# Attention on one core: the store of each pair in two halves of 64 rows, on both sides of the V load

## The chip, the core and the metric

The kernel runs on one core of a Trainium2 chip. The metric is the device time of one execution in microseconds (us), lower is better. Times shown are those of the unprofiled runs; a profiled execution has a time of its own, and its trace is where durations come from.

## What is computed

Attention with grouped heads, in bfloat16. 16 batches, 32 query heads of 16 positions, 8 key/value heads of 2048 positions, 128 elements per head; four query heads share one key/value head. Cut to what matters:

```
B, Hq, Hkv, Sq, Sk, D = 16, 32, 8, 16, 2048, 128
scores = einsum("bhqd,bhkd->bhqk", q, k) * D ** -0.5
out = einsum("bhqk,bhkd->bhqd", softmax(scores), v)
```

There are 16 x 8 = 128 key/value heads, each with 4 x 16 = 64 query rows. K and V together are 128 MB of input; the output is 2 MB.

## The kernel before

Two key/value heads make a *pair* p, 64 pairs in all: 128 query rows, and so 128 rows of output. All data is moved by DMAs that one engine, SP (SyncE), issues from its own queue. A DMA is cut into packets that 16 DMA engines move; each engine works through its own ring in the order of the issues. For a pair, SP issues

- K (`load_k`, issue at L187): 1 MB into one of 6 buffers `Kn`, in rows of 8 KB; before that it waits (`sem_kt`) until VectorE has transposed the pair that used the buffer;
- V (`load_v`, L195): 1 MB into one of 8 buffers `Vb`, in rows of 4 KB; before that it waits (`sem_pv`) for the product with V of the pair that used the buffer. The last pair's V comes in three pieces (L200), so that its product can begin early;
- the store (`store`, L213): 128 rows of 256 B, 32 KB, from one of 8 buffers `Osb` (in the profile `O`) to the output; before that it waits (`sem_nm`) until ACT has written the buffer;
- for every four pairs Q (`load_q`, L208), 128 KB.

The engines' part in a pair: VectorE (DVE) transposes K's blocks into `KT` (L343), takes the scores from PSUM with their minimum (L361) and the reciprocal of the sum of a row (L352). TensorE (PE) makes the scores (L274, L233), transposes the exponentials (L285) and multiplies by V (L302). ScalarE (ACT) takes the exponential (L391), copies the transposes out of PSUM (L401), and *norms* (L411): it scales the product by the reciprocal into `Osb`. Before a norm that reuses a buffer of `Osb`, ACT waits (`sem_o`) until the store from it, eight pairs earlier, has landed. GpSimd spreads Q (L176).

SP's order is written out by hand: a loop over steps t = 0 to 76. In step t it issues K of pair t, now and then Q, V of pair t-5 (`VLAG`), and the store of pair t-12 (`SLAG`):

```
for t in range(NP + SLAG + 1):
    if t < NP:
        load_k(t)
...
    if 0 <= t - VLAG < NP:
        load_v(t - VLAG)
    if 0 <= t - SLAG < NP:
        store(t - SLAG)
```

From step 64 on there is no K load left, from step 69 on no V load: the last eight steps hold stores only. At the very end SP waits until all stores have landed (L226). Each DMA adds 16 to its semaphore when it is complete, one for each of the 16 DMA engines.

Of the kernel before, what the change touches and what calls it, by code (L numbers as in the profile page):

```python
# [15 lines left out]
NO = 8  # L16
# [5 lines left out]
SLAG = 12  # L22
# [4 lines left out]
def bass_standalone__gqa_softmax__sampling_kernel(  # L27
# [11 lines left out]
    NP = G // 2  # L39
# [21 lines left out]
    Osb = [sb(f"O{i}", [128, 128], BF16) for i in range(NO)]  # L61
# [13 lines left out]
    sem_o = [sem(f"sem_o{i}") for i in range(NO)]  # L75
# [9 lines left out]
    sem_nm = sem("sem_nm")  # L85

    qf = q.rearrange("b h s d -> (b h s) d")
    of = out.rearrange("b h s d -> (b h s) d")
# [64 lines left out]
    def stage_ap(what):  # L153
        x = what[2] if what[0] == "P" else 2
        return ST_ps[:, 512 * x:512 * (x + 1)]

    def o_ap(p):
        if p < NP - 3:
            return O_ps[:, 0:128]
        x = p - (NP - 3)  # L160
        return S_ps[:, 512 * x:512 * x + 128]

    with nc.Block() as block:

        @block.gpsimd
        def _(gp):
            gp.iota(iota_t[:, :], [[1, 128]], base=0, channel_multiplier=-1).then_inc(sem_id, 1)
            gp.wait_ge(sem_id, 1)
            gp.tensor_scalar(ident[:, :], iota_t[:, :], 0.0, None, op0=ALU.is_equal).then_inc(sem_id, 1)
            gp.tensor_scalar(ident4[:, :], iota_t[:, :], 0.0, None, op0=ALU.is_equal).then_inc(sem_id, 1)  # L170
            for c in range(NQC):
                gp.wait_ge(sem_q[c % NQ], 16 * (c // NQ + 1))
                if c >= 1:
                    gp.wait_ge(sem_st, last_q[c - 1, 1] + 1)
                src = Qn[c % NQ][:, :, :].rearrange("p j (b x) -> p (j b) x", b=2)
                gp.tensor_copy(  # L176
                    Q4[:, :, :, :, :].rearrange("p j b r x -> p (j b) r x"),
                    src.unsqueeze(2).to_broadcast([128, 2 * QPAIRS, 4, 64]),
                ).then_inc(sem_q4, 1)

        @block.sync
        def _(sp):
            def load_k(p):
                s = p % NK
                if p >= NK:
                    sp.wait_ge(sem_kt, p - NK + 1)
                sp.dma_start(Kn[s][:, :], kf[p]).then_inc(sem_k[s], 16)  # L187

            def load_v(p):
                s = p % NV  # L190
                if p >= NV:
                    sp.wait_ge(sem_pv, p - NV + 1)
                if p < NP - 1:
                    dst = Vb[s][:, :, :, :].rearrange("a g j d -> a g (j d)")
                    sp.dma_start(dst, vf[:, 2 * p:2 * p + 2, :]).then_inc(sem_v[s], 16)  # L195
                    return
                for x, (lo, hi) in enumerate(zip(CUTS, CUTS[1:])):
                    dst = Vb[s][:, :, lo:hi, :].rearrange("a g j d -> a g (j d)")
                    src = vf[:, 2 * p:2 * p + 2, D * lo:D * hi]
                    sp.dma_start(dst, src).then_inc(sem_vl[x], 16)  # L200

            def load_q(c):
                s = c % NQ
                if c >= NQ:
                    sp.wait_ge(sem_q4, c - NQ + 1)
                rows = 128 * QPAIRS
                src = qf[rows * c:rows * (c + 1), :].rearrange("(a j) d -> a j d", j=QPAIRS)
                sp.dma_start(Qn[s][:, :, :], src).then_inc(sem_q[s], 16)  # L208

            def store(p):  # L210
                s = p % NO
                sp.wait_ge(sem_nm, p + 1)
                sp.dma_start(of[128 * p:128 * (p + 1), :], Osb[s][:, :]).then_inc(sem_o[s], 16)  # L213

            for t in range(NP + SLAG + 1):
                if t < NP:
                    load_k(t)
                for c in range(NQC):
                    if t == max(c, QPAIRS * c - QLEAD):
                        load_q(c)  # L220
                if 0 <= t - VLAG < NP:
                    load_v(t - VLAG)
                if 0 <= t - SLAG < NP:
                    store(t - SLAG)
            for s in range(NO):
                sp.wait_ge(sem_o[s], 16 * (NP // NO))  # L226

        @block.tensor
        def _(pe):
# [11 lines left out]
            def emit(op, at, v_at):  # L241

                if op[0] == "QT":
                    _, c, b, u = op
                    if b == 0:
                        pe.wait_ge(sem_q4, at(QPAIRS * c, QPAIRS))
# [6 lines left out]
                    ins.then_inc(sem_st, 1)  # L253
                elif op[0] == "S":
                    _, p = op
                    pe.wait_ge(sem_kt, at(p + 1))
                    if p >= 1:
# [19 lines left out]
                    ins.then_inc(sem_s, 1)  # L277
                elif op[0] == "PT":
                    _, p, h, u = op
                    if h == 0:  # L280
                        pe.wait_ge(sem_exp, at(p + 1))
# [91 lines left out]
        @block.scalar  # L373
        def _(act):
            for op in act_prog:
                if op[0] == "qe":
                    _, c, b, u = op
                    act.wait_ge(sem_st, u + 1)
                    if c >= 2 and b == 0:
                        act.wait_ge(sem_s, QPAIRS * (c - 1))  # L380
                    act.activation(  # L381
                        QT[c % 2][:, b, :].rearrange("p (a j) -> p a j", j=QPAIRS),
                        stage_ap(op).rearrange("p (j a) -> p a j", j=QPAIRS), ACT.Copy,
                    ).then_inc(sem_ev, 1)
                elif op[0] == "exp":
                    _, p = op
                    act.wait_ge(sem_max, p + 1)
                    if p >= 2:
                        act.wait_ge(sem_st, last_p[p - 2, 1] + 1)

                    act.activation(  # L391
                        P[p % 2][:, :].bitcast(BF16).rearrange("p (n y e) -> p n y e", n=16, e=2),
                        Sneg[p % 2][:, :].rearrange("p (n e y) -> p n y e", n=16, e=2), ACT.Exp,
                        bias=nbias[:, p:p + 1], scale=-1.0, accum_out=rowsum[:, p:p + 1],
                    ).then_inc(sem_exp, 1)
                elif op[0] == "pe":
                    _, p, h, u = op
                    act.wait_ge(sem_st, u + 1)
                    if h == 0 and p >= NPT:
                        act.wait_ge(sem_pv, p - NPT + 1)  # L400
                    act.activation(  # L401
                        PT[p % NPT][:, 4 * h:4 * (h + 1), :].rearrange("p t q -> p (t q)"),
                        stage_ap(("P", p, h)), ACT.Copy,
                    ).then_inc(sem_ev, 1)
                else:
                    _, p = op
                    act.wait_ge(sem_pv, p + 1)
                    act.wait_ge(sem_rec, p + 1)
                    if p >= NO:
                        act.wait_ge(sem_o[p % NO], 16 * (p // NO))  # L410
                    act.activation(Osb[p % NO][:, :], o_ap(p), ACT.Copy,  # L411
                                   scale=rrec[:, p:p + 1]).then_inc(sem_nm, 1)

# [27 lines left out]
```

## Time and profile before

| what | value |
|---|---|
| median of 3 runs | 341.77 us (341.57 to 341.88) |
| the profiled execution | 342.24 us |
| its span, from the first to the last instruction | 340.5 us |
| busy: DVE, PE, ACT, POOL | 295.3, 278.8, 267.0, 31.8 us |
| read from HBM, written to it | 136.31 MB, 2.10 MB |
| mean rate | 407 GB/s over the span |
| K, V, Q, store: median from issue to landing | 15.9, 16.4, 15.5, 15.4 us |

How to read what follows: PE, PEld, DVE, ACT, POOL and SP are the engines (PEld are TensorE's weight loads); a q behind the name (SPq) means the engine's queue of instructions. L187 is line 187 of the kernel before. `Vb<-in_v_dram` is a DMA from the input v into a buffer Vb; `x64` is a number of instructions. A row of tenths has 40 digits, one for each fortieth of the span, and 9 means 90% or more. q1 is the queue row in which all of SP's DMAs are; q8 and q14 carry the program's own instructions. The chain of waits is followed back from the last instruction: at each step to what released it. The trace also keeps a record of each DMA packet (start, duration, bytes), and of the time at which each DMA engine told a semaphore that its share had landed (here called landing records).

### The profile page before, as it was taken

The numbers are of one execution on the slowest core, as the hardware profiler recorded it, in microseconds if no ns is written. First come the engines' busy times: TensorE is split into PE (matmuls) and PEld (weight loads), VectorE is DVE, ScalarE is ACT, GpSimd is POOL, SyncE is SP. The second block draws the span as 40 slices with busy tenths as digits, with TensorE's granted clock in tenths as the row PEclk, the third lists the DMA queues.
The fourth block names the chain that finished last, engine by engine and source line by source line (L and its number), as shares of the span: only waits on it lengthen the run. The fifth ranks groups of instructions, "written<-read, shape, count | busy, mean of one in ns | idle before, by whom it ended". The sixth has DMA issues, their size and how long they took to land.

```text
span 340.5 us, 9888 instructions
## 1 busy us (share of the span) xinstructions
PE 278.8 (82%) x4736; PEld 161.6 (47%) x3712; DVE 295.3 (87%) x320; ACT 267.0 (78%) x353; POOL 31.8 (9%) x23
## 2 busy tenths in 40 slices
PE   0687999999998787888788797897878878888885
PEld 0233555555465445445355354454454454454454
DVE  2489999999999988989989889889889889899860
ACT  1178889999888786877878877887878869778785
POOL 3202020202010020200202011020200202000000
PEclk9979999999999999999999999999999999999999
DMA  8999999999999999999999999999999999999996
GB/s 295 398 418 416 410 414 409 414 415 415 416 418 415 416 417 417 415 419 417 416 418 412 420 418 413 420 416 417 420 413 418 414 416 420 419 415 420 416 409 205
DMA packets 38705, 138.63 MB, mean 407 GB/s; under 512 B 11552, under 2 KB 14112, under 8 KB 30496
## 3 DMA queue, kind: packets, MB, share of 16 engines
q1 hardware_dynamic: 38688, 138.43, 100.7%
q8 instruction: 8, 0.13, 0.2%
q14 instruction: 9, 0.07, 0.1%
HBM read 136.31 MB, written 2.10 MB: 407 GB/s over the span
## 4 chain that ended last, share of the span: by engine, by line
DMA 58%; DVE 16%; SPq 10%; issue 7%; PE 6%; ACT 1%; POOL 1%
DMA Vb<-in_v_dram 52%; DVE KT L343 11%; SPq L187 7%; DVE Sneg L361 5%; DMA Kn<-in_k_dram 5%; PE O_ps L302 3%; SPq L213 2%; DMA Qn<-in_q_dram 1%; ACT O L411 1%; PE S_ps L274 1%; PE S_ps L233 1%; SPq L195 1%; PE ST_ps L252 1%; POOL Q L176 1%; SPq L200 0%
## 5 line engine op out<-in xcount | busy, mean ns | idle before, releaser
L343 DVE STREAM_TRANSPOSE KT<-Kn 128x1024 f32<-128x1024 f32 x128 | 151.5, 1222 | 28.7 <-DMA Kn<-in_k_dram 28.7
L391 ACT ACTIVATE P<-Sneg,nbias 128x2048 bf16<-128x2048 f32 x64 | 159.6, 2493 | 6.0 <-DVE Sneg L361 6.0
L361 DVE TENSOR_SCALAR_CACHE_REDUCE Sneg<-S_ps 128x2048 f32<-128x2048 f32 x64 | 144.4, 2256 | 7.1 <-PE S_ps L233 7.1
L274 PE MATMUL S_ps<-KT,QT 32*64 32x512 bf16 x1024 | 105.7, 393 | 6.7 <-DVE Sneg L361 5.1
L233 PE MATMUL S_ps<-KT,QT 32*64 32x512 bf16 x1024 | 104.8, 388 | 0.0
L302 PE MATMUL O_ps<-Vb,PT 128*64 128x128 bf16 x1952 | 66.2, 221 | 38.0 <-DMA Vb<-in_v_dram 38.0
L302 PEld LDWEIGHTS O_ps<-Vb,PT 128*64 128x64 bf16 x1952 | 56.5, 110 | 80.4 <-issue 43.5
L401 ACT ACTIVATE PT<-ST_ps 128x512 f32<-128x512 f32 x128 | 69.5, 595 | 19.2 <-PE ST_ps L285 19.2
L285 PE MATMUL ST_ps<-ident,P 128*128 128x128 f32 x512 | 70.5, 281 | 4.7 <-ACT P L391 4.3
L274 PEld LDWEIGHTS S_ps<-KT,QT 32*64 32x64 bf16 x1024 | 32.4, 104 | 71.0 <-issue 60.3
L285 PEld LDWEIGHTS ST_ps<-ident,P 128*128 128x128 f32 x512 | 55.3, 141 | 13.9 <-ACT P L391 9.6
L176 POOL COPY Q<-Qn 128x2048 bf16<-128x2048 bf16 x16 | 30.3, 1893 | 255.9 <-PE ST_ps L252 252.0
L411 ACT ACTIVATE O<-O_ps,rrec 128x128 bf16<-128x128 f32 x61 | 22.5, 369 | 35.1 <-PE O_ps L302 35.0
L252 PE MATMUL ST_ps<-ident,Q 128*128 128x128 f32 x128 | 20.2, 282 | 8.8 <-POOL Q L176 8.1
L381 ACT ACTIVATE QT<-ST_ps 128x512 f32<-128x512 f32 x32 | 19.3, 603 | 8.5 <-PE ST_ps L252 8.5
L252 PEld LDWEIGHTS ST_ps<-ident,Q 128*128 128x128 f32 x128 | 15.5, 145 | 9.2 <-issue 8.1
L391 ACT ACTIVATION_READ_ACCUMULATOR P<-Sneg,nbias 128x1 f32 x64 | 13.2, 207 | 0.0
L352 DVE RECIPROCAL rrec<-rowsum 128x1 f32<-128x1 f32 x64 | 10.2, 159 | 3.0 <-ACT P L391 3.0
L361 DVE DVE_READ_ACCUMULATOR Sneg<-S_ps 128x1 f32 x64 | 5.3, 84 | 0.0
L302 PE MATMUL S_ps<-Vb,PT 128*64 128x128 bf16 x96 | 3.6, 221 | 1.1 <-issue 0.6
L302 PEld LDWEIGHTS S_ps<-Vb,PT 128*64 128x64 bf16 x96 | 2.9, 110 | 1.9 <-issue 1.5
L411 ACT ACTIVATE O<-S_ps,rrec 128x128 bf16<-128x128 f32 x3 | 1.1, 369 | 2.0 <-PE S_ps L302 2.0
(8 smaller groups left out, 3.0 us busy)
## 6 DMA issues: line engine op xcount, KB each, us to landing
Kn<-in_k_dram SPq DMA_DIRECT2D x64, 1024.0 KB, 15.9
Vb<-in_v_dram SPq DMA_DIRECT2D x63, 1024.0 KB, 16.4
Qn<-in_q_dram SPq DMA_DIRECT2D x16, 128.0 KB, 15.5
out_dram<-O SPq DMA_DIRECT2D x64, 32.0 KB, 15.4
Vb<-in_v_dram SPq DMA_DIRECT2D x1, 512.0 KB, 12.6
Vb<-in_v_dram SPq DMA_DIRECT2D x1, 320.0 KB, 12.3
Vb<-in_v_dram SPq DMA_DIRECT2D x1, 192.0 KB, 12.4
```

What stands on the lines that cost most here:

```text
L176: gp.tensor_copy(Q4[:, :, :, :, :].rearrange("p j b r x -> p (j b) r x"), src.unsqueeze(2).to_broadcast([128, 2 * QPAIRS, 4, 64]),).then_i ...
L187: sp.dma_start(Kn[s][:, :], kf[p]).then_inc(sem_k[s], 16)
L233: return pe.add_instruction(mybir.InstMatmult(name=nc.get_next_instruction_name(), engine=mybir.EngineType.PE, ins=[pe.lower_ap(rhs), pe.l ...
L252: ins = pe.transpose(dst[:, 128 * j:128 * (j + 1)], src[:, j, b, :], ident4[:, :])
L274: ins = pe.matmul(s_ap, w, x, start=(acc == 0), stop=(acc == 3))
L285: ins = pe.transpose(dst[:, 128 * t:128 * (t + 1)], P[p % 2][:, 128 * x:128 * (x + 1)], ident4[:, :])
L302: ins = pe.matmul(o_ap(p)[64 * g:64 * (g + 1), :], pt[:, j // 2, j % 2, 64 * g:64 * (g + 1)], Vb[p % NV][:, g, j, :], start=(j == 0), stop ...
L343: ins = dve.transpose(KT[p % NKT][:, :].rearrange("p (t b e a x) -> p x e t b a", t=J // 2, b=2, e=2, x=2)[:, x, :, :, :, :], Kn[p % NK][: ...
L361: dve.tensor_scalar(Sneg[p % 2][:, :].rearrange("p (t h x) -> p h t x", t=8, h=2), S_ps[:, :].rearrange("p (h t x) -> p h t x", t=8, h=2), ...
L391: act.activation(P[p % 2][:, :].bitcast(BF16).rearrange("p (n y e) -> p n y e", n=16, e=2), Sneg[p % 2][:, :].rearrange("p (n e y) -> p n ...
L401: act.activation(PT[p % NPT][:, 4 * h:4 * (h + 1), :].rearrange("p t q -> p (t q)"), stage_ap(("P", p, h)), ACT.Copy,).then_inc(sem_ev, 1)
L411: act.activation(Osb[p % NO][:, :], o_ap(p), ACT.Copy, scale=rrec[:, p:p + 1]).then_inc(sem_nm, 1)
```

## The change

The store of a pair becomes two DMAs of 64 rows each. The first half waits for the norm, as the store did, and is issued behind K (and Q) and before V; the second half is issued behind V, where the store was, and waits for nothing of its own. In the steps without a V load the two halves follow each other. As a pair's two halves count on the same semaphore, the waits on `sem_o`, ACT's and SP's last one, count 32 for each use of a buffer in place of 16.

```diff
-            def store(p):
+            def store(p, x):
                 s = p % NO
-                sp.wait_ge(sem_nm, p + 1)
-                sp.dma_start(of[128 * p:128 * (p + 1), :], Osb[s][:, :]).then_inc(sem_o[s], 16)
+                if x == 0:
+                    sp.wait_ge(sem_nm, p + 1)
+                sp.dma_start(of[128 * p + 64 * x:128 * p + 64 * (x + 1), :],
+                             Osb[s][64 * x:64 * (x + 1), :]).then_inc(sem_o[s], 16)
...
+                if 0 <= t - SLAG < NP:
+                    store(t - SLAG, 0)
                 if 0 <= t - VLAG < NP:
                     load_v(t - VLAG)
                 if 0 <= t - SLAG < NP:
-                    store(t - SLAG)
+                    store(t - SLAG, 1)
             for s in range(NO):
-                sp.wait_ge(sem_o[s], 16 * (NP // NO))
+                sp.wait_ge(sem_o[s], 32 * (NP // NO))
...
                     if p >= NO:
-                        act.wait_ge(sem_o[p % NO], 16 * (p // NO))
+                        act.wait_ge(sem_o[p % NO], 32 * (p // NO))
```

## The prediction

> **What bounds the kernel now.** I read the page's DMA rows first, because the chain of waits gives 58% to DMA. Parts 2 and 3 of the page (tenths in 40 slices; packets; time of the queue's packets as a share of 16 engines' span):
>
> ```profile
> DMA  8999999999999999999999999999999999999996
> DMA packets 38705, 138.63 MB, mean 407 GB/s; under 512 B 11552, under 2 KB 14112, under 8 KB 30496
> q1 hardware_dynamic: 38688, 138.43, 100.7%
> ```
>
> From the second slice to the last but one all 16 DMA engines are busy, and the time of the packets exceeds the span. VectorE, the next busiest, is at 87%. So every packet that goes on an engine's ring ahead of the last V load moves the end, and everything else is covered, unless it leaves a ring empty.
>
> The 11552 packets under 512 B tell what a DMA costs beside its data: 64 stores of 128 rows are 8192 packets of 256 B, and the other 3360 are 210 issues (64 K, 63 V whole and 3 pieces, 16 Q, 64 stores) x 16: one small packet per DMA and engine, which tells the semaphore.
>
> The DMA view from 60 to 320 us, the even stretch:
>
> ```profile
> DMA packets 29620, 108.35 MB, mean 417 GB/s; under 512 B 8984, under 2 KB 10343, under 8 KB 23192
> q1 hardware_dynamic: 29612, 108.26, 102.5%
> ```
>
> Packets overlap a little. 102.5% of 260 us is 266.5 us of packet time per engine, 6.5 us too much; 29612/16 = 1851 packets share it, 3.5 ns each. The packet records of the trace (start, duration, bytes) give mean durations in this stretch: semaphore packet 9.1 ns, 256 B 18.1, 1 KB 46.0, 4 KB (V) 161.5, 8 KB (K) 309.5. Less 3.5, a semaphore packet holds its engine for 5.6 ns and a row of a store for 14.6.
>
> Then SP, which the change lengthens. Its timeline (start, duration):
>
> ```profile
> 194.69 0.44 SPq L195 DMA_DIRECT2D Vb<-in_v_dram  x1
> 195.17 3.62 SPq L213 DMA_DIRECT2D out_dram<-O  x1
> 198.83 1.72 SPq L187 DMA_DIRECT2D Kn<-in_k_dram  x1
> 200.60 1.18 SPq L195 DMA_DIRECT2D Vb<-in_v_dram  x1
> 201.82 1.11 SPq L213 DMA_DIRECT2D out_dram<-O  x1
> 202.98 2.15 SPq L187 DMA_DIRECT2D Kn<-in_k_dram  x1
> ```
>
> The issues stand 0.04 us apart and take anything from 0.43 to 4 us: SP is held because the rings are full, not by a semaphore. The view of SP's waits says otherwise (71.4 us at L213 for ACT's L411), and is not to be believed: the store at 201.82 is the 31st, and the 31st norm ended on ACT at 181.46, 20 us earlier. A DMA lands 15.6 us (median) after its issue, some three pairs of work later: the rings are never near empty.
>
> The end, from the chain in order of time:
>
> ```profile
> 325.36 12.36 DMA Vb<-in_v_dram
> 337.72 0.04 issue
> 337.76 0.38 PE S_ps L302 x6
> 338.14 0.02 issue
> 338.16 0.37 ACT O L411
> ```
>
> The last piece of V lands at 337.72; six matmuls, the norm, and at 338.56 the last store's issue (0.33 us in SP's timeline; shortest time to landing 1.4 us) follow, up to 340.5.
>
> **The change, part by part.** The sum is made against the profiled execution: 342.24 us, of which 340.5 are the span. The runs' median is 341.77; I add the sum to that.
>
> (a) *One more DMA per pair.* Rows and bytes are the same. 64 rows divide by 16, so I take each half as 4 rows and one semaphore packet on every engine. Ahead of the last V load stand both halves of pairs 0 to 55: 56 more semaphore packets per engine x 5.6 ns = 0.31 us. Bounds: nothing, and 9.1 x 56 = 0.51 us if the packet overlaps nothing.
>
> (b) *Half of store 56 moves ahead of the last V load.* In the last step with a V load the store stood wholly behind it. 4 x 14.6 + 5.6 = 64 ns, 0.06 us; at most 4 x 18.1 + 9.1 = 0.08.
>
> (c) *The last store is issued in two.* Nothing covers it. The shortest issue is 0.33 us for a store (32 KB), for Q (128 KB) and for K (1 MB), so it doesn't shrink with the size, and 0.05 us lies between two issues. The second half starts 0.38 us later and has 4 rows fewer to move per engine (4 x 14.6 = 0.06): +0.32 us. Bounds 0.31 and 0.38.
>
> (d) *SP's time:* one more issue per pair, 0.43 to 0.5 us when not held. Costed at nothing: K, V and a store take 1.4 us unheld in a pair of 5.1 us, and the full rings hide the rest. If a ring could run dry, the 0.5 us would count 64 times; with 15 us in the queue it can't.
>
> (e) *The wait on sem_nm now stands before V(t-5).* Queued behind it are V, the other half and the next K. While K loads last, the wait was over 20 us earlier (31st norm). In the tail, where no K load paces SP, the last V piece group is issued at 323.85; the norm that it would now wait for, the 57th, starts at 315.33 and takes 0.37: 8.1 us to spare. Nothing.
>
> (f) *ACT's wait for the output buffer* now needs both halves. The second keeps the place of the old store. Store 45 is issued at 278.31 and lands by 296.2 even with the longest time (17.9 us); the norm that reuses its buffer starts at 300.1. Nothing, with 3.9 us to spare.
>
> Sum: 0.31 + 0.06 + 0.32 = **0.69 us**: 342.93 for a profiled execution, **342.46** for the runs, and by the bounds (0 + 0.06 + 0.31 and 0.51 + 0.08 + 0.38) 342.14 to 342.74. A measurement of this kernel can tell about 0.2% from no change, 0.68 us, or 342.45. So the forecast stands on that line.
>
> **The rivals.**
>
> *A, the semaphore packets cost nothing.* They may fit into gaps that the engine has anyway, or a half may use only 8 engines, so that no packet is added. Then (a) is 0: 342.15. For it: nearly all of them are 9 ns beside a load of 2.5 us. Against: their time is in the 102.5% like any other's. [...]
>
> *B, a store's completion isn't covered.* Price from the tail: the stores queued behind the last V land 0.172 us after each other on one engine (landing records: seven on the last engine from 337.90 to 338.93), while 8 x 14.6 + 5.6 make 0.122. If each added half cost that 0.05 us, 56 would give 2.8 us, in place of (a): 344.95, slower. It decides where small DMA follows small DMA. Against: each half is now followed by a load of some 2.5 us, and in the even stretch a store and the K behind it land together 2.571 us after the V (0.186 and 2.385), no more than their packets' net time, so the load covers the completion.
>
> *C, half the partitions are read at half the rate.* The trace holds no DMA of 64 partitions. If every row of a half took 14.6 ns more, that is 8 x 57 x 14.6 ns = 6.7 us: 349.1. Against: the 16 engines are up to 3 us apart in the same DMA (landing records), and an engine's four rows take 0.06 us, so two of them seldom meet. [...]
>
> *D, faster: V's packets get shorter.* Their commonest duration is 159 ns against a mean of 161.5; over 63 x 16 per engine the excess is 2.5 us. Should bursts of writes cause it, and halved bursts halve it, 1.25 us come back: 341.2. Against: V packets that overlap 1 to 15 store packets exceed 159 ns by 2.0 to 2.4 ns, those that overlap none by 2.5 (by 4.6 beside more, a twentieth of all).
>
> **How the numbers follow.** Forecast 64%: 342.46, 342.1 to 342.75, with a little over half above the line of 342.45, since what I may have left out (one instruction packet more for SP's longer program, 0.31 us on one engine) can only add: 36% over, 28% under. A 12%, 342.15, under. B 10%, C 4%, over. D 10%, faster. That makes slower 50%, same 40%, faster 10%. The range reaches down to D's 341.2 and up to 342.74 + 0.31 + 0.11 (the runs' scatter) = 343.2; B and C stay out, 14%.
>
> **What would show it.** The page should have 39712 packets on q1 (+1024) and 12576 under 512 B; 38688 again speaks for A's 8 engines. 256 B packets at 18 ns refute C, 30 ns would bear it out. The period of the pairs should grow by 6 ns; 50 ns is B. The last store's two issues should stand 0.38 us apart, and SP's stores keep norms done long before. I'd be wrong altogether if SP's timeline showed gaps, or the DMA row a slice under 9 in the middle: a ring ran dry.

## The result and the profile after

The changed kernel takes 343.05 us (median of 5 runs, 342.68 to 343.80) against 341.72 us: a ratio of 1.0040, 95% interval 1.0029 to 1.0051, slower by 1.33 us. The forecast was 342.46, slower by 0.69. The profiled execution took 342.74 us, near the low end of its runs; its span is 341.0 us, against 340.5 before.

The page after, parts 2 and 3 (the same rows as before):

```profile
DMA  7999999999999999999999999999999999999993
DMA packets 39729, 138.63 MB, mean 407 GB/s; under 512 B 12576, under 2 KB 15136, under 8 KB 31520
q1 hardware_dynamic: 39712, 138.43, 100.1%
```

The counts are those forecast: 1024 packets more on q1, all under 512 B, 16 for each of the 64 added DMAs: a semaphore packet on each of 16 engines. That a half's 64 rows are 4 on each is the prediction's division; the packet records name no engine. The engines are still full: 9 in 38 of the 40 slices, 100.1% for q1. But the last slice has fallen from 6 to 3: the engines are done earlier, and the end is later. The end of the chain, in order of time:

```profile
324.75 11.13 DMA Vb<-in_v_dram
335.88 0.04 issue
335.92 0.47 PE S_ps L306 x10
336.39 0.04 issue
336.43 0.38 PE S_ps L306 x6
336.81 0.02 issue
336.83 0.37 ACT O L415
```

The last piece of V lands at 336.38 by its landing records, in place of 337.72, and the last norm ends at 337.20 in place of 338.53. So the loads *gained* 1.33 us between these two profiled executions; the one before, 342.24, lies 0.5 us above the median of its runs, and a typical gain is smaller (0.81 in e1 below). From the last norm to the end of the span it is 3.76 us in place of 1.94: 1.82 us were lost behind it. The difference of the spans, 0.49 us, is what is left of two effects of opposite sign.

Where the 1.82 us went, the stores' issues in the last stretch tell. From 329 us on, the kernel before and then the kernel after (duration in ns: shortest, median, longest; first and last start):

```profile
L213 SPq DMA_DIRECT2D out_dram<-O x8: 332/379/1801, 329.0 to 338.6; - x8
```

```profile
L214 SPq DMA_DIRECT2D out_dram<-O x14: 594/596/1312, 329.0 to 338.7; - x14
```

A whole store takes 0.33 us when SP is free; none of these halves takes less than 0.594. Fourteen of them stand back to back. In the kernel before, SP's last store is issued 0.03 us after the norm:

```profile
338.56 0.33 SPq L213 DMA_DIRECT2D out_dram<-O  x1
```

In the kernel after, SP's timeline has four halves in one piece where the last norm ends on ACT:

```profile
336.74 2.51 SPq L214 DMA_DIRECT2D out_dram<-O  x4
336.83 0.37 ACT L415 ACTIVATE O<-S_ps,rrec 128x128 bf16<-128x128 f32 x1 [1.41 <-PE S_ps L306]
```

At 337.20, when the last output is ready, SP is still with the halves of the pair before; the last half is issued from 338.65 to 339.25.

### The profile page after: what moved, and what is told of

Read it like the earlier page. It is cut to its first block, busy times and chain, and to the rows that moved or that the text cites. A ratio compares the mean times of both kernels' runs of the same rounds, so it can differ in the third digit from the quotient of the medians.

```text
span 341.0 us, 9952 instructions
## 1 busy us (share of the span) xinstructions
PE 278.5 (82%) x4736; PEld 161.2 (47%) x3712; DVE 295.4 (87%) x320; ACT 267.0 (78%) x353; POOL 31.8 (9%) x23
## 3 DMA queue, kind: packets, MB, share of 16 engines
q1 hardware_dynamic: 39712, 138.43, 100.1%
## 4 chain that ended last, share of the span: by engine, by line
DMA 47%; SPq 23%; DVE 16%; issue 8%; PE 4%; ACT 0%
DMA Vb<-in_v_dram 35%; SPq L214 13%; DMA Kn<-in_k_dram 11%; DVE KT L347 11%; SPq L187 5%; DVE Sneg L365 5%; SPq L195 4%; PE O_ps L306 2%; PE S_ps L278 1%; PE S_ps L237 1%; SPq L208 1%; DVE rrec L356 0%; PE S_ps L306 0%; ACT O L415 0%; SPq L200 0%
## 5 line engine op out<-in xcount | busy, mean ns | idle before, releaser
L395 ACT ACTIVATE P<-Sneg,nbias 128x2048 bf16<-128x2048 f32 x64 | 159.6, 2494 | 6.0 <-DVE Sneg L365 6.0
```

The lines of the kernel that those rows point to most:

```text
L395: act.activation(P[p % 2][:, :].bitcast(BF16).rearrange("p (n y e) -> p n y e", n=16, e=2), Sneg[p % 2][:, :].rearrange("p (n e y) -> p n ...
```

## Experiments

Theory T: the loss is SP's queue in the tail. A half takes 0.60 us to issue, 0.64 with the gap, and the 15 that stand behind the last V load (of pair 56 only the second half does) outlast the last norm, from 328 us on. Rival S: the stream pays, through more packets. A second question was whether the shorter V packets (159.6 ns after, 161.5 before) belong to the change.

### e1: halves in the stream, whole stores in the tail

```diff
             def store(p, x):
                 s = p % NO
+                if p >= NP - NO:
+                    if x == 1:
+                        sp.wait_ge(sem_nm, p + 1)
+                        sp.dma_start(of[128 * p:128 * (p + 1), :], Osb[s][:, :]).then_inc(sem_o[s], 16)
+                    return
...
```

> Halves for pairs 0 to 55, one whole store for each of the last eight pairs. Theory T (the tail's issues): in the changed kernel's profile a half store takes 0.60 us to issue with others behind it, so 16 of them hold SP from 329 to 339.25 us, 2.05 us beyond the last norm (337.20). With 8 whole stores SP is free when the last norm ends, and the end is that of the stream: if the stream is as in the changed kernel's profile (last V at 336.39 against 337.72 before) 340.4 to 340.8 us; if that early V was chance, 341.7 + 0.31 for 56 semaphore packets = 342.0. Rival S (the stream pays: more packets, shorter queues): the tail doesn't matter, and the time stays at 342.7 to 343.1.

Measured: 340.95 us against 341.76, ratio 0.9977 (0.9968 to 0.9986). It beats both kernels. The end of its chain, and SP's last issue in its timeline:

```profile
336.46 0.38 PE S_ps L311 x6
336.84 0.02 issue
336.87 0.37 ACT O L420
```

```profile
337.26 0.33 SPq L215 DMA_DIRECT2D out_dram<-O  x1
```

V lands as early as in the changed kernel, and the store goes out 0.02 us after the norm. The span ends at 339.17, 1.93 us behind the norm, as before. T holds, S falls, and V's packets (159.5 ns) are short again.

### e2: whole stores in the stream, halves in the tail

```diff
             def store(p, x):
                 s = p % NO
+                if p < NP - NO:
+                    if x == 1:
+                        sp.wait_ge(sem_nm, p + 1)
+                        sp.dma_start(of[128 * p:128 * (p + 1), :], Osb[s][:, :]).then_inc(sem_o[s], 16)
+                    return
...
```

> Whole stores for pairs 0 to 55, halves for the last eight. Theory T: the stream is that of the kernel before, but SP issues 16 halves at 0.64 us from 329.0 us on and is at the last one about 339.4 in place of 338.56, so the end moves by 1.0 to 1.4 us: 342.7 to 343.1. Rival S: only the last store's second issue counts, 0.3 us: 342.0 to 342.1. The issues of the last halves should stand 0.64 us apart with no wait between them.

Measured: 344.23 us, ratio 1.0063 (1.0049 to 1.0077). Halves in the tail alone cost 2.47 us, more than T's 1.0 to 1.4. The stores' issues in the tail:

```profile
L219 SPq DMA_DIRECT2D out_dram<-O x15: 466/596/1613, 328.9 to 340.2; - x15
```

The mechanism is T's, the size was too small: SP's issues ran on to 340.77, 2.58 us behind the last norm (338.19). Three of the 15 took longer, 1.61, 0.90 and 1.38 us, which the reckoning of 0.64 each had not; why, no run shows. From the last norm to the end it is 4.27 us in place of 1.94. V's packets are at 161.9 ns, as in the kernel before.

### e3: the whole store between K and V

```diff
-                if 0 <= t - VLAG < NP:
-                    load_v(t - VLAG)
                 if 0 <= t - SLAG < NP:
                     store(t - SLAG)
+                if 0 <= t - VLAG < NP:
+                    load_v(t - VLAG)
```

> The whole store of 128 rows moved between K and V, nothing split: the change's move alone. In the changed kernel V's packets of 4 KB average 159.4 ns in the even stretch, before 161.5, which is 2.1 us over 63 V loads. If the place of the store between K and V does it, V's packets are at 159.4 here too and the time is 339.8 to 340.5. If the halving does it, or chance, they stay at 161.5 and the time is 341.7 + 0.12 (the store of pair 56 ahead of the last V) = 341.8.

Measured: 342.07 us, ratio 1.0011 (1.0002 to 1.0020). V's packets are at 159.7 ns, but K's are at 312.9 in place of 309.5: the lengthening has moved from V to K. Neither expectation had that. The place alone gains nothing.

### e4: the changed kernel again

> The changed kernel once more, unchanged, for a second profile. Theory T: its time is 342.7 to 343.8 as in the first five runs, and the last half is issued about 2 us after its norm again. If V's shorter packets (159.4 ns) belong to the change, they are there again; if they are chance, the mean lies elsewhere, up to 161.5.

Measured: 342.81 us, ratio 1.0029 (1.0017 to 1.0040); V's packets 159.4 ns, last norm 337.11, last half issued until 339.13. Both effects are the change's own. Against e1 on the same chip, the halves in the tail cost 1.86 us.

### e5: both halves behind V

e1, with the two halves next to each other:

```diff
-                if 0 <= t - SLAG < NP:
-                    store(t - SLAG, 0)
                 if 0 <= t - VLAG < NP:
                     load_v(t - VLAG)
                 if 0 <= t - SLAG < NP:
+                    store(t - SLAG, 0)
                     store(t - SLAG, 1)
```

> As the kernel with halves for pairs 0 to 55 and whole stores for the last eight (340.95 us), but both halves behind V, one right after the other. If the stream gains because the 8 rows of a store per DMA engine are torn in two bursts of 4 with a load between them, the gain goes: V's 4 KB packets are back at about 161.5 ns and the time is 341.76 + 0.31 = 342.1. If it gains from the form of the DMA (64 rows), V stays at 159.5 ns and the time at 341.0.

Measured: 342.04 us against 341.84, ratio 1.0006 (0.9997 to 1.0015); V at 161.5 ns. So the form of the DMA gains nothing; the load between the halves does. This also prices the 56 added DMAs with their semaphore packets: 0.20 us (-0.1 to 0.5), where the prediction had 0.31. Tearing the halves apart is worth 1.0 us (0.9977 against 1.0006).

### e6: the issue time by itself

Behind the end of the kernel before, series of six issues, each series begun when all DMAs ahead of it had landed:

```diff
...
+            series = [(0, 128, 0, 128), (0, 64, 0, 128), (64, 128, 0, 128), (0, 32, 0, 128),
+                      (0, 16, 0, 128), (0, 128, 0, 64)]
+            for n, (lo, hi, c0, c1) in enumerate(series):
+                for s in range(6):
+                    r = 128 * (NP - NO + s)
+                    sp.dma_start(of[r + lo:r + hi, c0:c1], Osb[s][lo:hi, c0:c1]).then_inc(sem_x[n], 16)
+                sp.wait_ge(sem_x[n], 96)
+            for n, hi in enumerate((128, 64), len(series)):
+                for s in range(6):
+                    sp.dma_start(Kn[s][0:hi, :], kf[s][0:hi, :]).then_inc(sem_x[n], 16)
+                sp.wait_ge(sem_x[n], 96)
```

> The kernel before, and behind its end eight series of six DMAs each, issued back to back with empty rings (stores of finished rows again, then K loads again): stores of 128, 64 (0 to 63), 64 (64 to 127), 32 and 16 rows, 128 rows of 128 B, loads of 128 and of 64 rows of 8 KB. Only the issue durations count. Known: 0.33 to 0.43 for 128 rows, 0.60 for 64 rows in the changed kernel's tail. If the number of rows decides, both series of 64 rows and the load of 64 rows take 0.60, and 128 rows of 128 B take 0.43; if the smaller bytes decide, 128 rows of 128 B take 0.60 too; if it is the place (rows 64 to 127), only that series does. 32 and 16 rows tell whether it goes on rising.

The eight series in this order (the two of K last; shortest, median, longest in ns):

```profile
L233 SPq DMA_DIRECT2D out_dram<-O x6: 332/432/432, 339.6 to 341.8; - x6
L233 SPq DMA_DIRECT2D out_dram<-O x6: 564/596/597, 343.4 to 346.5; - x6
L233 SPq DMA_DIRECT2D out_dram<-O x6: 467/596/597, 348.4 to 351.5; - x6
L233 SPq DMA_DIRECT2D out_dram<-O x6: 352/421/423, 353.3 to 355.6; - x6
L233 SPq DMA_DIRECT2D out_dram<-O x6: 314/420/428, 357.0 to 359.2; - x6
L233 SPq DMA_DIRECT2D out_dram<-O x6: 351/432/433, 360.7 to 363.0; - x6
```

```profile
L237 SPq DMA_DIRECT2D Kn<-in_k_dram x6: 340/436/661, 364.5 to 367.0; - x6
L237 SPq DMA_DIRECT2D Kn<-in_k_dram x6: 522/596/597, 381.7 to 384.8; - x6
```

Back to back, 64 rows take 0.596 us, in either half, as a store of 256 B rows or a load of 8 KB rows; 128, 32 and 16 rows take 0.42 to 0.44. It is neither the bytes nor a rise towards fewer rows. Why 64 differs stays open.

### e7: no stores in the stream

The stores of pairs 0 to 55, and ACT's wait for the buffer, are left out.

```diff
+                if p < NP - NO:
+                    return
                 sp.wait_ge(sem_nm, p + 1)
...
```

> The kernel before without the stores of pairs 0 to 55 (their rows of the output stay unwritten; ACT's wait for the buffer is left out too). If whole stores lengthen the load packets near them, V's 4 KB packets fall from 161.5 ns to 159.0 to 159.5 and the time is 341.76 less 56 x 0.122 = 6.8 and less 2.0 to 2.5: 332.4 to 333.0. If V's length has another cause, it stays at 161.5 and the time is 334.9.

Measured: 339.29 us, ratio 0.9924 (0.9909 to 0.9939). The theory in it fell: without stores V's packets are *longer*, 163.3 ns, and K's too, 315.1. Its DMA view from 60 to 320 us:

```profile
DMA packets 22664, 107.73 MB, mean 414 GB/s; under 512 B 1787, under 2 KB 3124, under 8 KB 16243
q1 hardware_dynamic: 22656, 107.65, 102.0%
```

The engines are as full as before (102.0%, 102.5% before), with fewer packets. 56 stores of 0.122 us, the prediction's estimate, are 6.8 us of each engine's time, and 2.55 us were saved: the longer loads took an estimated 64 x 8 x 5.6 ns + 63 x 16 x 1.8 ns = 4.7 us back. So stores don't lengthen loads here: the loads are longest in the kernel whose stream has no stores.

### e8: the tail on two queues

```diff
+                if x == 1 and p >= NP - NO:
+                    return
...
                                    scale=rrec[:, p:p + 1]).then_inc(sem_nm, 1)
+                    if p >= NP - NO:
+                        act.wait_ge(sem_nm, p + 1)
+                        act.dma_start(of[128 * p + 64:128 * (p + 1), :],
+                                      Osb[p % NO][64:128, :]).then_inc(sem_o[p % NO], 16)
```

> The changed kernel, but for the last eight pairs the second half is issued by ACT behind its norm, on its own queue. If the 0.64 us per half is the time of SP's own sequencer, SP has 8 halves in the tail and is free when the last norm ends: 340.9 to 341.3, as with whole stores. If it is a generator that both queues share, the 16 halves still take 0.64 us each and the end stays at 342.7 to 343.1. ACT's own work in the tail grows by 8 issues, which may cost up to 0.6 us where they stand before a copy that TensorE waits for.

Measured: 342.35 us, ratio 1.0019 (1.0010 to 1.0028), between the two expectations. SP is no longer late: both halves of the last pair go out at 338.39, SP's taking 0.47 us and ACT's 0.50 beside it, so there they don't wait for each other; at 334.67 both took 0.96. But ACT's issues stand in its own queue, and the last norm ends at 338.36 in place of 337.20. Whether the two queues share anything that an issue needs, this run doesn't tell.

### e9: halves by columns

```diff
-                sp.dma_start(of[128 * p + 64 * x:128 * p + 64 * (x + 1), :],
-                             Osb[s][64 * x:64 * (x + 1), :]).then_inc(sem_o[s], 16)
+                sp.dma_start(of[128 * p:128 * (p + 1), 64 * x:64 * (x + 1)],
+                             Osb[s][:, 64 * x:64 * (x + 1)]).then_inc(sem_o[s], 16)
```

> The changed kernel with the halves cut the other way: 128 rows of 128 B each, one half between K and V, one behind V, the last eight pairs too. An issue of 128 rows takes 0.43 us back to back, one of 64 rows 0.60 (series measured by itself). If the tail is lost to the issue time, 16 issues at 0.47 from about 328 us end before the last norm and SP is free for the last pair: its second half is issued within 0.4 to 0.6 us of the norm's end, and the tail is as with whole stores but for that, 0.3 to 0.5 us. If it is the mere number of issues, it stays 2 us late. The stream: if what shortens the loads is that a store stands on both sides of V, V's 4 KB packets are at 159.5 ns again; 16 packets of 128 B in place of 8 of 256 B cost an unknown 0 to 0.07 us per pair and engine. Together 341.2 to 342.0 by the first theory, plus up to 2 us if the small packets cost in full; by the second at least 343.

Measured: 343.13 us, ratio 1.0036 (1.0024 to 1.0048). By the total alone it fits both theories; the trace tells them apart. The store issues from 332 us on:

```profile
L214 SPq DMA_DIRECT2D out_dram<-O x15: 333/432/2078, 330.4 to 339.6; - x15
```

The same number of issues, 0.43 us each, and SP is free in time: the last norm ends at 339.17, the first half follows at 339.19, the second at 339.57, and the span ends 2.38 us behind the norm, 0.44 more than before, where the 64-row halves lost 1.82. In the stream the small packets cost more: one of 128 B takes 13.0 ns, 9.5 less the prediction's 3.5 of overlap, and (16 x 9.5 - 8 x 14.6) x 57 = 2.0 us, an estimate. Against that the loads are the shortest of all kernels (159.2 and 309.2 ns), which gives back an estimated 63 x 16 x 2.2 + 64 x 8 x 0.3 ns = 2.4 us. The two nearly cancel, so most of the 0.9 us that are left of the 1.34 is not accounted for.

### e10: whole stores two by two

```diff
-                if 0 <= t - SLAG < NP:
-                    store(t - SLAG)
+                p = t - SLAG
+                if 0 <= p < NP - 8 and p % 2 == 1:
+                    store(p - 1)
+                if NP - 8 <= p < NP or 0 <= p < NP and p % 2 == 1:
+                    store(p)
```

(and 16 output buffers)

> The kernel before with whole stores, but issued two by two, every second pair, behind V (16 output buffers in place of 8, so that ACT doesn't wait; the last eight pairs one by one). Bytes, packets and issues are those of before. In the trace of before, loads are long (3.0 ns over the shortest on average) where no engine had a store in the microsecond before, and short (0.8 ns) where stores were dense; without stores at all V's packets are 163.3 ns and K's 315.1. If loads are long because all 16 engines load at once, the store-free stretches are longer here, the excess per load packet rises by a quarter or more, and the time is 342.2 to 343.3. If a store costs what its packets take, wherever it stands, the time is 341.7 to 341.9.

Measured: 343.03 us, ratio 1.0036 (1.0023 to 1.0050). Same bytes, packets and issues as before, only bunched: 1.24 us slower. The last V lands at 338.31 in place of 337.72.

### The loads, kernel by kernel

From the packet records between 60 and 320 us: mean durations in ns; the mean time of a load packet over the shortest common one (159 and 309 ns; the few over by 60 or more left out); and the share of load packets with no store packet on any engine in the microsecond before their middle.

| kernel | V, 4 KB | K, 8 KB | mean excess | store-free share |
|---|---|---|---|---|
| e7, no stores | 163.3 | 315.1 | 4.73 | 100% |
| e10, two by two | 161.5 | 312.1 | 2.48 | 66% |
| e2, halves in the tail | 161.9 | 309.7 | 1.96 | 47% |
| e5, both halves behind V | 161.5 | 309.6 | 1.67 | 44% |
| before | 161.5 | 309.5 | 1.61 | 26% |
| e3, whole between K and V | 159.7 | 312.9 | 1.58 | 22% |
| after | 159.6 | 310.1 | 0.50 | 0% |
| e1, halves, whole in the tail | 159.5 | 309.7 | 0.34 | 0% |
| e9, column halves | 159.2 | 309.2 | 0.02 | 0% |

The streams of e4 and e8 are that of the changed kernel, and they have 0.35 and 0.36 at 0%. In the kernel before, the packets of the store-free stretches are 3.0 ns over, the others 1.1. The engines are some 3 us apart in a DMA (2.90 us, median, from a load's first landing record to its last in the kernel before) and a pair takes 5.2, so a burst of stores behind V leaves a stretch in which all 16 engines load, 26% of the load packets; with a burst every 2.5 us there is always one that stores (0%). e7 and e10 changed the share on purpose, and time and excess followed; e10's was expected. And e2 issues the same stream as the kernel before, yet has the larger share in its profile, and the larger excess with it.

A second reading stands beside this one: that a load is short when a store stands directly ahead of it in SP's order. In the kernel before, K, directly behind the store, is over by only 0.7 ns even where no engine stored, and V, behind K, by 1.8 even where one did. In e3, where V stands behind the store, V is over by 0.2 beside stores and 2.4 without, K by 2.8 and 5.3. Both seem to count; halves on both sides of V change both, and no run separates them. That loads are longer because all 16 engines load at once is read from the table's order, not shown; what would make them longer, no run shows.

## Why the prediction was right or wrong

The direction was right, the size half: 0.69 of 1.33 us (1.05 in e4). That the number came so near is in good part luck. The loads gained 1.0 us (e1 against e5) that the sum did not have, and the tail lost 1.86 where the sum had 0.32: two errors of opposite sign.

- **What bounds the kernel: right, but its rule was too strong.** The engines are full (q1 at 100.7% of the span before, 100.1% after). That every packet ahead of the last V load moves the end is false: e7 took an estimated 6.8 us of packets away and saved 2.55.
- **(a) The semaphore packets: fits, not proven.** 0.31 forecast, 0.20 (-0.1 to 0.5) in e5, an interval that includes zero.
- **(b) Half of store 56 ahead of the last V:** not seen by itself; at 0.06 us no run could. e3, where the whole store stood there, was 0.3 us slower in all.
- **(c) The last store's two issues: this step failed.** It held that an issue doesn't shrink with its size, from issues that all had 128 rows, and put 0.38 us behind a free SP. 64 rows take 0.60, and SP isn't free: measured 1.82 us in the profile, 1.86 against e1, where the step had 0.32.
- **(d) SP's time at nothing: right in the stream, wrong in the tail.** The step named its cover, full rings and 15 us of queue. The queue is measured (15.6 us from a store's issue to its landing in the stream before); that full rings held SP was the author's reading of the issue times, 0.455 to 4.18 us for a store there. In the tail, behind the last V load, that cover is gone: the last four halves land 1.8 to 1.9 us after their issue, and SP's own issues are the queue. The step looked at the stream alone. Halves in the tail alone cost 2.47 us in e2, (c) and (d) together.
- **(e), (f) The moved wait and ACT's wait: right.** Before the last V piece at 325.59 the 57th norm had been done since 314.61, and SP's longest wait for a norm in the changed kernel is 0.8 us. The view of ACT's waits in the changed kernel has none for a store.
- **Rival A** (packets free): the counts rule out 8 engines; whether the 0.20 us (-0.1 to 0.5) of e5 is 0 isn't told.
- **Rival B** (completion uncovered): wrong. Between the 11th and the 51st V load the time fell by 12 ns per pair (206.84 us against 207.31), where B had 50 ns more. Such stretches differ by more from profile to profile (208.58 in e2, with the stream of before); the firmer answer is e5, where 56 added halves cost 0.20 us and not 2.8.
- **Rival C** (half rate for half the partitions): wrong; a 256 B packet takes 18.0 ns in halves of 64 rows, and 18.1 in the whole stores of before.
- **Rival D** (V's packets get shorter): its event came, 159.6 ns and 1.0 us gained, close to its 1.25, but for another reason. It blamed bursts of writes; e7 shows that loads are longer without them. The evidence that the prediction held against it, that packets beside stores are no longer than others, was read as no effect, where it was the trace of the opposite one.

## What to carry to other kernels

Cost an added issue in each stage by itself: here 56 added halves in the stream cost 0.20 us (-0.1 to 0.5, e5), and the eight added in the tail, where the last stores wait behind one another in SP's queue, 1.86 us (e4 against e1). Take an issue's price from the shape that will be issued, or measure it, and not from the nearest sizes: here 64 rows took 0.596 us, 128 and 32 rows 0.42 to 0.44. With all DMA engines busy, the sum of packet times wasn't the bound here (e7: an estimated 6.8 us less, 2.55 saved): look at whether loads stretch in stretches without stores (3.0 ns over the shortest there, 1.1 elsewhere, in the kernel before), and try spreading the small transfers evenly between the loads. Here that gave 340.95 us, against 341.76, once the tail kept whole stores.

## What the runs showed of the hardware that was not expected

- In e6 an issue of 64 rows held SP for 0.596 us back to back, one of 128, 32 or 16 rows 0.42 to 0.44, for stores of 256 B rows and, at 64 and 128 rows, for loads of 8 KB rows alike.
- In the kernel whose stream has loads alone (e7) K's 8 KB packets took 315.1 ns and V's 4 KB 163.3; with column halves of stores spread through the stream (e9) 309.2 and 159.2.
- A store packet of 128 B took 13.0 ns (e9), one of 256 B 18.0 (after).
